# Batch setup in pieces, finer pacing of table work, and 512-column inverse groups with two accumulators in a fused attention and long-convolution kernel

## The chip, the cores and the metric

The kernel runs on one core of one Trainium2 chip. The metric is the device time of one execution in microseconds (us). Executions of one kernel on one chip agree within some 1%; three chips were used, and on two of them the kernel before is 0.5 to 0.9% slower than on the first (medians 3187.9, then 3214.7 to 3217.6, and 3204.8). So kernels are compared here by ratio to the kernel before in the same rounds, or stage by stage in the traces.

## The reference, cut to what matters

```python
def _attn_ref(u, v, z):                    # u, v: 8 x 3136 x 256, z: 8 x 3136 x 64
    scores = (1.0 / S) * np.matmul(z, z.transpose(0, 2, 1))
    attn = np.maximum(scores, 0.0) ** 2
    return u * np.matmul(attn, v)

def _moe_ref(x, w_proj, filter_fft, w_out):
    x1, x2, x3 = split(x @ w_proj)         # three parts of 256 columns
    X2 = np.fft.rfft(x2, n=S, axis=1)      # 1569 frequencies
    H = np.fft.rfft(filter_fft, n=S, axis=0)[None]
    y = x1 * np.fft.irfft(X2 * H, n=S, axis=1) * x3
    return y @ w_out                       # float32
```

The attention result is the x of the second function. Both Fourier transforms are done as matmuls with tables of cosines and sines, which the kernel makes itself while attention runs.

## The kernel before

A sequence of 3136 rows is 25 tiles of 128 rows (the last has 64) and 7 chunks of up to 512 columns (the last has 64). 1569 frequencies are 13 tiles (the last has 33 rows). The attention stage of a batch starts with a setup:

```python
for b in range(B):
    zT16 = batchp.tile([dqk, S], BF16, name="zT16")
    for t in range(NST):                                   # 25 tiles
        zsb = io.tile([P, dqk], F32, name="zblk")          # two buffers
        nc.sync.dma_start(out=zsb[:rows, :], in_=z[b, ds(t * P, rows), :])
        ptz = psA_pr.tile([P, CH], F32, name="ps_pr")
        nc.tensor.transpose(ptz[:dqk, :rows], zsb[:rows, :], ...)
        nc.vector.tensor_copy(zT16[:, ds(t * P, rows)], ptz[:dqk, :rows])
    # ... the same for u, two transposes per tile, copied by ScalarE
    # ... v: 25 loads on the GpSimd queue into the only buffer v16
```

Then come the chunks. After each, table work is given out in whole "slices": a slice is one band of 128 table rows, or the start or end of a group of four bands.

```python
    for c in range(NC):
        for kt in range(NST):
            nc.tensor.matmul(ps[...], zT16[...], zT16[...], start=True, stop=True)   # scores
            R = rring.tile([P, CH], F32, name="Rblk")
            nc.scalar.activation(R[...], ps[...], AF.Relu)
            if kt % ACT_SQUARE_EVERY == (ACT_SQUARE_EVERY - 1):      # every fourth
                nc.scalar.activation(A16[:krows, kt, :cw], R[...], AF.Square)
            else:
                nc.vector.tensor_tensor(A16[:krows, kt, :cw], R[...], R[...], ALU.mult)
            for dh in range(2):
                nc.tensor.matmul(psout[:, dh, :cw], v16[...], A16[:, kt, :cw], ...)
        # the gate: xT (name xTch) = psout * u, by VectorE; it ends the chunk
        # ... projections of xT, evicted by ScalarE and VectorE into ev tiles
        #     of two buffers (xiT, x2blk) and stored
        emit_table_slices(slices_per_chunk)   # one slice: done after 39 of 56 chunks
```

The inverse transform, for each half of four batches:

```python
CHI = 256
psB_i = phb.enter_context(tc.tile_pool(name="psB_i", bufs=1, space=PSUM))
for c in range(NCI):                          # 12 chunks of 256 columns, one of 64
    # ... loads itC on the sync queue and itS on the scalar queue, one DMA per
    #     frequency tile: 26 DMAs into pools of two buffers
    for bl in range(Bh):                      # 4 batches
        for dh in range(2):
            po = psB_i.tile([P, CHI], F32, name="psB_inv")
            for ft in range(NFT):             # 13: one accumulation group has 26 matmuls
                nc.tensor.matmul(po, Ac16[:fw, ft, ...], itC[:fw, ft, :cw], ...)
                nc.tensor.matmul(po, As16[:fw, ft, ...], itS[:fw, ft, :cw], ...)
            # gt = po * g1 and yT2 = gt * g3 by VectorE
        # ... output matmuls (psB_out), evicted by ScalarE (ostage), stored
```

## Time and profile before

| | kernel before |
|---|---|
| time, median of 5 runs | 3185.91 us (3182.3 to 3203.1) |
| attention with tables | 1580 us |
| forward transform and inverse, first half | 425 and 415 us |
| forward transform and inverse, second half | 336 and 428 us |

The whole-span line of busy times on the page of the kernel before is the place where one starts, and alone it misleads: PE (TensorE) looks like the bound everywhere and everything else like slack.

```profile
PE 2771.3 (87%) x15356; PEld 1356.8 (43%) x15356; DVE 1608.1 (51%) x3669; ACT 1327.4 (42%) x3400; POOL 132.4 (4%) x235
```

DVE is VectorE, ACT is ScalarE, POOL is GpSimd, PEld is the weight loads; each has its busy microseconds, share and number of instructions. The 51% of VectorE is an average over an attention stage where it is at 80% and two inverse stages where it is at 19%.

For finer comparisons this document marks the stages by instructions: attention ends at the last gate; an inverse is counted from its first to its last emptying of an accumulator (the instruction that writes gt); what lies between is put down to the forward transform. These marks give 1578.6, 435.7, 405.7, 346.3 and 412.5 us for the kernel before. The windows of the prediction (1580, 425, 415, 336, 428) count the filling of the first group into the inverse.

### The profile page before, as it was taken

The page shows a single profiled execution, that of the slowest core. Times are in us where ns is not written, and L with a number is a line of the kernel's source. Part 1 is how long each engine was busy: PE and PEld are TensorE (multiplying, and loading weights), DVE is VectorE, ACT ScalarE, POOL GpSimd, SP SyncE. Part 2 cuts the span into 40 slices and gives each one's busy share as a digit, 9 for nine tenths or more (in the row PEclk, how much of TensorE's full clock was granted, in tenths as well). Part 3 has the DMA queues.
Part 4 walks back from the last instruction along what each step waited for, and adds up shares of the span by engine and source line. Part 5 has one row for each costly group of instructions (what it writes and reads, how often), then busy time and mean ns, then how long its engine had stood idle before and what let it go on. Part 6 is the DMA issues. An engine that isn't in the chain of part 4 may idle for free.

```text
span 3183.3 us, 45398 instructions
## 1 busy us (share of the span) xinstructions
PE 2771.3 (87%) x15356; PEld 1356.8 (43%) x15356; DVE 1608.1 (51%) x3669; ACT 1327.4 (42%) x3400; POOL 132.4 (4%) x235
## 2 busy tenths in 40 slices
PE   8979979899798897989869999888888888888888
PEld 2333333333333332323334554566664333466666
DVE  8989988889989765655512222211111222311111
ACT  7879878788687775867600000000000000000000
POOL 2010010100101001010100000000000000000000
PEclk9989988899798899989979999999999999899999
DMA  4142243331332423222253221534344333234333
GB/s 91 61 110 82 87 91 109 69 123 44 87 107 64 111 61 59 66 50 69 62 132 58 49 57 26 142 108 122 106 111 130 61 61 61 60 102 120 107 108 82
DMA packets 552881, 271.08 MB, mean 85 GB/s; under 512 B 268236, under 2 KB 540104, under 8 KB 552648
## 3 DMA queue, kind: packets, MB, share of 16 engines
q1 hardware_dynamic: 352320, 200.91, 22.2%
q10 hardware_dynamic: 167960, 52.28, 7.3%
q0 software_dynamic: 32368, 14.99, 3.9%
q8 instruction: 120, 1.97, 0.3%
q14 instruction: 113, 0.93, 0.1%
HBM read 179.32 MB, written 103.59 MB: 89 GB/s over the span
## 4 chain that ended last, share of the span: by engine, by line
PE 68%; DMA 12%; ACT 8%; DVE 8%; issue 2%; ACTq 1%; SPq 0%; POOL 0%; DVEq 0%; POOLq 0%
PE psoutT L245 16%; PE psB_fwd L344 9%; PE psB_fwd L346 9%; PE ps_sc L234 9%; PE psB_inv L401 7%; PE psB_inv L403 6%; ACT Rblk L237 4%; DMA itC<-tabCi 3%; PE ps_pr L257 2%; DMA itS<-tabSi 2%; DVE gt L410 2%; DVE A L241 2%; PE pt_tab L167 2%; DMA zblk<-in_z_dram 2%; PE ps_pr L215 1%
## 5 line engine op out<-in xcount | busy, mean ns | idle before, releaser
L237 ACT ACTIVATE Rblk<-ps_sc 128x512 f32<-128x512 f32 (+2 forms) x1400 | 713.4, 546 | 201.9 <-PE ps_sc L234 190.7
L245 PE MATMUL psoutT<-A,v 128*128 128x512 bf16 (+1 forms) x2800 | 736.4, 368 | 29.5 <-DVE A L241 19.0
L241 DVE TENSOR_TENSOR A<-Rblk 128x512 bf16<-128x512 f32 (+2 forms) x1064 | 637.4, 621 | 182.4 <-ACT Rblk L237 173.5
L401 PE MATMUL psB_inv<-itC,Ac 128*128 128x256 bf16 (+2 forms) x2704 | 617.5, 273 | 85.7 <-DVE gt L410 81.2
L403 PE MATMUL psB_inv<-itS,As 128*128 128x256 bf16 (+2 forms) x2704 | 616.7, 273 | 2.2 <-DMA itS<-tabSi 2.0
L344 PE MATMUL psB_fwd<-x2h,bandc 128*128 128x512 bf16 (+2 forms) x1300 | 507.8, 391 | 66.7 <-DVE As L356 33.2
L346 PE MATMUL psB_fwd<-x2h,bands 128*128 128x512 bf16 (+2 forms) x1300 | 506.2, 389 | 0.0
L234 PE MATMUL ps_sc<-zT 64*128 64x512 bf16 (+2 forms) x1400 | 459.4, 368 | 41.1 <-ACT Rblk L237 30.6
L410 DVE TENSOR_TENSOR gt<-psB_inv,g 128x256 bf16<-128x256 f32 (+1 forms) x208 | 85.2, 410 | 669.3 <-PE psB_inv L403 601.7
L420 ACT ACTIVATE ostage<-psB_out 128x256 f32<-128x256 f32 (+1 forms) x200 | 76.8, 384 | 760.8 <-PE psB_out L418 484.6
L245 PEld LDWEIGHTS <-v 128*128 128x128 bf16 x2800 | 233.5, 101 | 313.7 <-issue 196.1
L355 ACT ACTIVATE Ac<-psB_fwd 128x512 bf16<-128x512 f32 (+1 forms) x52 | 31.0, 597 | 720.9 <-PE psB_fwd L346 704.7
L356 DVE CAST As<-psB_fwd 128x512 bf16<-128x512 f32 (+1 forms) x52 | 35.9, 691 | 578.3 <-ACT Ac L355 578.3
L403 PEld LDWEIGHTS <-As 128*128 128x128 bf16 (+1 forms) x2704 | 263.0, 100 | 128.0 <-issue 96.7
L401 PEld LDWEIGHTS <-Ac 128*128 128x128 bf16 (+1 forms) x2704 | 262.0, 99 | 105.3 <-issue 70.8
L234 PEld LDWEIGHTS <-zT 64*128 64x128 bf16 (+1 forms) x1400 | 104.1, 95 | 336.9 <-issue 281.3
L344 PEld LDWEIGHTS <-bandc 128*128 128x128 bf16 (+2 forms) x1300 | 130.3, 100 | 180.7 <-DMA bandc<-tabC 31.8
L346 PEld LDWEIGHTS <-bands 128*128 128x128 bf16 (+2 forms) x1300 | 130.1, 100 | 164.4 <-issue 45.5
L239 ACT ACTIVATE A<-Rblk 128x512 bf16<-128x512 f32 (+1 forms) x336 | 194.9, 580 | 1.5
L221 POOL DMA_DIRECT2D v<-in_v_dram x200 | 116.3, 639 | 1291.0 <-DVE xTch L250 915.2
L418 PE MATMUL psB_out<-wo,yT 128*128 128x256 bf16 (+1 forms) x400 | 97.0, 282 | 42.2 <-ACT ostage L420 40.7
L257 PE MATMUL ps_pr<-xTch,wp 128*128 128x512 bf16 (+1 forms) x448 | 120.0, 361 | 10.3 <-DVE xTch L250 3.9
(74 smaller groups left out, 2407.8 us busy)
## 6 DMA issues: line engine op xcount, KB each, us to landing
ublk<-in_u_dram SPq DMA_DIRECT2D x192, 128.0 KB
out_dram<-ostage SPq DMA_DIRECT2D x192, 128.0 KB
bands<-tabS ACTq DMA_DIRECT2D x576, 32.0 KB
bandc<-tabC SPq DMA_DIRECT2D x576, 32.0 KB
itC<-tabCi SPq DMA_DIRECT2D x288, 64.0 KB
itS<-tabSi ACTq DMA_DIRECT2D x288, 64.0 KB
v<-in_v_dram POOLq DMA_DIRECT2D x192, 64.0 KB, 3.1
x1T_d<-xiT SPq DMA_DIRECT2D x96, 128.0 KB
```

The source lines that it names most:

```text
L221: nc.gpsimd.dma_start(out=v16[:rows, t, :], in_=v[b, ds(t * P, rows), :])
L234: nc.tensor.matmul(ps[:krows, :cw], zT16[:, ds(kt * P, krows)], zT16[:, ds(s0, cw)], start=True, stop=True)
L237: nc.scalar.activation(R[:krows, :cw], ps[:krows, :cw], AF.Relu)
L239: nc.scalar.activation(A16[:krows, kt, :cw], R[:krows, :cw], AF.Square)
L241: nc.vector.tensor_tensor(A16[:krows, kt, :cw], R[:krows, :cw], R[:krows, :cw], ALU.mult)
L245: nc.tensor.matmul(psout[:, dh, :cw], v16[:, kt, ds(dh * P, P)], A16[:, kt, :cw], start=(kt == 0), stop=(kt == NST - 1))
L257: nc.tensor.matmul(pp[:, :cw], wp16[:, ksub, ds((comp * 2 + nb) * P, P)], xT[:, ksub, :cw], start=(ksub == 0), stop=(ksub == 1))
L344: nc.tensor.matmul(pacc[:fw, 0, cN, :cwN], bandc[:rows, t, :fw], x2h[:rows, t, ds(cN * CH, cwN)], start=(t == 0), stop=(t == NST - 1))
L346: nc.tensor.matmul(pacc[:fw, 1, cN, :cwN], bands[:rows, t, :fw], x2h[:rows, t, ds(cN * CH, cwN)], start=(t == 0), stop=(t == NST - 1))
L401: nc.tensor.matmul(po[:, :cw], Ac16[:fw, ft, ds(col0, P)], itC[:fw, ft, :cw], start=(ft == 0), stop=False)
L403: nc.tensor.matmul(po[:, :cw], As16[:fw, ft, ds(col0, P)], itS[:fw, ft, :cw], start=False, stop=(ft == NFT - 1))
L410: nc.vector.tensor_tensor(gt[:, :cw], po[:, :cw], g1[:, :cw], ALU.mult)
```

## The change

Its intent is to take the serial batch start off the path, to spread the table work evenly over attention, and to halve the number of accumulation groups in the inverse and free each from the wait for its predecessor. The core of the diff:

```diff
-        vpool = pha.enter_context(tc.tile_pool(name="vpool", bufs=1))
+        vpool = pha.enter_context(tc.tile_pool(name="vpool", bufs=2))
+        batchin = pha.enter_context(tc.tile_pool(name="batchin", bufs=2))
+        evy = pha.enter_context(tc.tile_pool(name="evy", bufs=4))   # x2blk
+        evx = pha.enter_context(tc.tile_pool(name="evx", bufs=4))   # xiT
 ... a band is now yielded in three parts: columns 0-511, 512-1023, the rest
-                    yield gen_band
+                    yield first
+                    yield (lambda f=gen_block: f(CH))
+                    if not last:
+                        yield fin
 ... setup of batch b+1, one piece of four tiles per chunk of batch b
+        NPACE = B * NC - 4                                  # 52
+        def setup_piece(b, tiles, g):
+            nc.sync.dma_start(out=zin[:, :nf, :], in_=z[b, r, :].rearrange("(t p) d -> p t d", p=P))
+            nc.sync.dma_start(out=uin[:, :nf, :], in_=u[b, r, :].rearrange("(t p) d -> p t d", p=P))
+            nc.gpsimd.dma_start(out=v16[:, t0:t0 + nf, :], in_=v[b, r, :].rearrange("(t p) d -> p t d", p=P))
+            # ... then the same transposes and copies as before, for four tiles
-                emit_table_slices(slices_per_chunk)
+                if b + 1 < B:
+                    setup_piece(b + 1, nxt, c)
+                k = b * NC + c + 1
+                want = min(3 * NST, ceil(3 * NST * k / NPACE))
+                emit_table_slices(want - emitted[0])
+                emitted[0] = want
 ... second half
-    CHI = 256
+    CHI = 512
-        psB_ff, psB_i and psB_o, one buffer each, open through both halves
+        psB_ff only in the first forward stage; in the inverse stage:
+                    psB_i = ph4.enter_context(tc.tile_pool(name="psB_i", bufs=2, space=PSUM))
+                    psB_o = ph4.enter_context(tc.tile_pool(name="psB_o", bufs=1, space=PSUM))
+                    if h == 1:                              # forward stage of the second half
+                        padp = ph3.enter_context(tc.tile_pool(name="padp", bufs=1))
+                        padt = padp.tile([P, 2 * CH], F32, name="padt")
+                        nc.vector.memset(padt[:, 0:1], 0.0)
-                            ost = outstage.tile([P, 2, D], F32, name="ostage")
+                            ost = outstage.tile([P, 4, D], F32, name="ostage")
```

The pad shifts the two band buffers of the second forward stage past the memory that the last inverse chunk's tables still hold, so that their loads may start before that inverse ends.

## The prediction

> **What bounds the kernel now.** I first cut the span into its five stages, with the table of stretches. The attention stage, with projections and table generation, ends at about 1580 us (the last chunk's gate is at 1578.6). Then come forward transform and inverse of the first half of the batches, and the same for the second half.
>
> ```profile
> core 0: us, PE busy (x) PEld busy (x) DVE busy (x) ACT busy (x) POOL busy (x), PEclk, DMA share, GB/s
> 0.00:1580.00 1580.00, 1391.83 (x6293) 511.93 (x6294) 1270.61 (x3022) 1215.39 (x3133) 120.00 (x212) 0.92 0.30 79
> 1580.00:2005.00 425.00, 369.74 (x1956) 194.22 (x1955) 90.61 (x113) 18.90 (x40) 12.36 (x24) 0.92 0.33 66
> 2005.00:2420.00 415.00, 349.49 (x2903) 257.84 (x2903) 79.88 (x218) 38.80 (x101) 0.00 (x0) 0.98 0.44 117
> 2420.00:2756.00 336.00, 299.87 (x1302) 129.91 (x1301) 87.03 (x101) 14.71 (x25) 0.00 (x0) 0.95 0.33 70
> 2756.00:3184.00 428.00, 360.41 (x2905) 262.88 (x2904) 79.98 (x218) 39.57 (x102) 0.00 (x0) 0.94 0.39 107
> ```
>
> The reader sees half of the time in attention, with no engine full over the whole stage, and 843 us in the two inverses, with VectorE and ScalarE nearly idle. Second, the same view in 50 us stretches shows that attention is three regimes, not one:
>
> ```profile
> 550.00:600.00 50.00, 48.80 (x248) 17.76 (x245) 47.70 (x116) 43.66 (x112) 0.00 (x0) 1.00 0.16 54
> 750.00:800.00 50.00, 47.93 (x213) 16.21 (x211) 47.06 (x108) 42.46 (x102) 0.00 (x0) 1.00 0.16 54
> 950.00:1000.00 50.00, 48.13 (x210) 16.09 (x209) 47.89 (x108) 44.42 (x105) 0.00 (x0) 1.00 0.14 48
> 1000.00:1050.00 50.00, 28.99 (x171) 14.28 (x169) 44.22 (x143) 29.55 (x105) 15.56 (x25) 0.57 0.55 121
> 1150.00:1200.00 50.00, 48.65 (x198) 15.31 (x198) 33.47 (x53) 40.68 (x82) 0.00 (x0) 1.00 0.11 35
> ```
>
> Where tables are made (up to about 1100 us) VectorE is 94 to 96% busy. A batch start (1000 to 1050) has PE at 29 of 50 and clock 0.57. After the tables are done (1150), VectorE has a third of its time free. Third, the timeline of VectorE gives the chunk period through the gate that ends each chunk (the instruction writing xTch); here the last small chunk of batch 6 and the first four chunks of batch 7:
>
> ```profile
> 1397.55 0.36 DVE L250 SCALAR_TENSOR_TENSOR xTch<-psoutT,uT 128x64 bf16<-128x64 f32 x2 [0.31 <-PE psoutT L245]
> 1445.72 1.28 DVE L250 SCALAR_TENSOR_TENSOR xTch<-psoutT,uT 128x512 bf16<-128x512 f32 x2
> 1471.44 1.29 DVE L250 SCALAR_TENSOR_TENSOR xTch<-psoutT,uT 128x512 bf16<-128x512 f32 x2 [0.28 <-PE psoutT L245]
> 1499.85 0.69 DVE L250 SCALAR_TENSOR_TENSOR xTch<-psoutT,uT 128x512 bf16<-128x512 f32 x1 [0.37 <-PE psoutT L245]
> 1522.78 1.28 DVE L250 SCALAR_TENSOR_TENSOR xTch<-psoutT,uT 128x512 bf16<-128x512 f32 x2
> ```
>
> The first chunk takes 48.2 us, a plain one 22.9. The cause stands in the PE timeline of the batch before: loads of z of one tile each, through two buffers, ahead of every transpose.
>
> ```profile
> 1227.31 0.39 PE L205 MATMUL ps_pr<-ident_f,zblk 128*64 128x128 f32 x1 [3.20 <-DMA zblk<-in_z_dram]
> 1228.14 0.39 PE L205 MATMUL ps_pr<-ident_f,zblk 128*64 128x128 f32 x1 [0.44 <-DVE zT L206]
> ```
>
> Fourth, for the inverse, the PE timeline at the end of an accumulation group:
>
> ```profile
> 2201.99 0.27 PE L403 MATMUL psB_inv<-itS,As 128*128 128x256 bf16 x1
> 2202.19 0.28 PE L401 MATMUL psB_inv<-itC,Ac 33*128 33x256 bf16 x1
> 2202.31 0.27 PE L403 MATMUL psB_inv<-itS,As 33*128 33x256 bf16 x1
> 2202.51 0.28 PE L418 MATMUL psB_out<-wo,yT 128*128 128x256 bf16 x1
> 2203.09 0.27 PE L401 MATMUL psB_inv<-itC,Ac 128*128 128x256 bf16 x1 [0.30 <-DVE gt L410]
> ```
>
> Matmuls start 0.11 us apart, lose about 0.1 us at each change to and from the 33-row block, and the next group waits for VectorE to empty the only accumulator.
>
> **What the Trainium skill says.**
> - "TensorE: Matmul & The Clock Gate", section "Back-to-back issue gap": a warm matmul of N columns follows the last after N / 2.4 + 2.5 ns, so 109 ns for 256 columns and 216 ns for 512. The trace agrees: 0.109 us in the inverse, 0.215 in attention. So wide matmuls win nothing per column; what they halve is the number of group ends.
> - The same page, section "Part 1: The HAM clock gate": a PE idle for some 3.4 us falls to half clock. The clock of 0.57 in the batch start above agrees.
> - "Perfetto Trace Analysis", section "Optimization Strategy": regimes with different busiest engines gain from being interleaved. That is the intent of the new pacing; the stretches at 950 and 1150 are two such regimes.
> - The same page, section "Matmuls": independent groups should rotate through PSUM banks so that the emptying of one overlaps the next. The 0.30 above and 0.52 us at the next group are that wait.
>
> **The change, part by part.**
>
> Attention, batch setup: z, u and v come four tiles per transfer, one piece per chunk of the batch before, with v in two buffers. The work of setup stays (600 fp32 transposes, 400 ScalarE and 200 VectorE copies); its serial wait goes, save for batch 0. The seven first chunks of batches 1 to 7 took 47.3, 49.1, 53.1, 52.3, 57.5, 46.7 and 48.2 us, together 354. If each becomes an ordinary chunk with its share of setup, about 27 us, this saves 354 - 7 x 27 = 165 us: 1579 - 165 = 1414.
>
> Attention, pacing: the same table work in thirds of a band over 52 chunks, not whole bands in the first 39 of 56. It removes no instruction. What bounds the evened stage is the sum per engine: VectorE 1270.6 us, at the 95.1% of the three full stretches (47.55 of 50), needs 1336; ScalarE 1215.4 at their 87.0% (43.51 of 50) needs 1397. The two counts are not added: they are two views of the same stage.
>
> Attention, output buffers of four: ScalarE and VectorE waited 35.8 and 9.3 us in the list of waits for stores of the projected tiles. Part of this comes back. Batch 0 keeps its start (first gate at 47.1 us), now with u queued between the z loads: about 10 us lost. I choose 1405 us, between the counts, saving 174.
>
> Forward stages: only the place of the filter accumulator and a 4 KB pad change, which keeps the band tiles clear of the larger inverse tables so that they still load early. 426 and 336 us stay.
>
> Inverse, per half: six chunks of 512 columns and one of 64, in place of twelve of 256 and one. Now a pair of groups takes 3.62 + 4.04 = 7.66 us: 2 x (26 x 0.109 + 0.20) + 4 x 0.109 = 6.5, and 1.16 of waits for the accumulator. With two accumulators the waits go: a pair at 512 columns is 2 x (26 x 0.216 + 0.20) + 8 x 0.109 = 12.5 us, a chunk of four batches 50.0, six of them 300. To this come:
> - the start: the first group needs all tables of its chunk, now 3.2 MB; at the 211 GB/s of 2010 to 2020 us that is 15 us, and the group ends some 2 us later, so about 11 us over the group's own 5.8. Now it is about 7 (first emptying 9.6 us after the first load).
> - the ends of chunks. Now the ScalarE queue issues 13 table loads at 0.5 to 0.65 us each when a chunk's tables come free, its evictions of the output stand behind them, and PE loses about 2 to 4 us: chunks are 32 to 34 us apart, not 30.6. I estimate 4 us for each of five larger bursts: 20.
> - the 64-column chunk, 12.6 us now (2407.4 to 2420.0): 12.
>
> Sum 343; with 3 more in the first half, where the band loads compete, and 1 at the very end, 346 and 344, for 415 and 428 now.
>
> Total: 1405 + 426 + 346 + 336 + 344 = 2857 us, a saving of about 328 us or 10%.
>
> **The rivals.**
> - *Setup stalls PE in order.* The transposes now stand inside full chunks, and share two PSUM buffers with the projections. If a load or a copy is late, scores behind it wait. For it: the PE order is fixed, and VectorE, which empties z, is nearly full. Against it: a piece has a whole chunk (25 us) for 1.2 MB, and the DMA share mid-batch is 0.14 to 0.16. Three microseconds in each of 48 chunks would make about 3000.
> - *The inverse turns its accumulator wait into a table wait.* The bytes of a burst double, and both issuing queues also carry the gates and outputs. For it: the DMA share at such a chunk end (2178 to 2189) is already 0.73. Against it: a chunk now lasts 50 us, and 7.6 MB in it is 152 GB/s. If bursts cost 12 us each, 40 us per half: about 2935.
> - *Better overlap than counted.* With VectorE at 95% from start to end attention takes 1340 to 1350, and with no chunk-end loss the inverses 325: about 2755.
>
> **Range and chances.** Attention I hold to within 55 us either way, the two inverses together to within 45; mostly independent, so about 75 around 2857, stretched upward for the PE stalls: 2775 to 2950. All three rivals stay faster by over 2% (3122 us); only both bad ones together, doubled, would reach it. Faster 0.97, same 0.02, slower 0.01.
>
> **What would show it.** Attention should end near 1405 with no first chunk over 35 us after batch 0, VectorE near 90% and ScalarE near 87% all along, no stretch of clock 0.57. If chunks are all longer with VectorE under 85%, the in-order rival holds. In the inverse the gap before a group for VectorE should fall from 81 us to almost nothing, groups should end about 5.8 to 6.7 us apart, and losses should sit at chunk ends alone. The forward stages should keep their length; a longer second forward stage would show that the pad fails and bands load late. The prediction is wrong if attention stays over 1480 or an inverse over 375.

## The result, and the profile after

The changed kernel takes 2863.39 us (median of 9 runs, 2857.99 to 2869.07); the kernel before took 3187.89 on that chip (16 runs, 3180.23 to 3203.44). The ratio is 0.8976, with a 95% interval of 0.8960 to 0.8992. A ratio is the mean time of one kernel's fast runs over that of the other's of the same rounds, so not quite the ratio of the medians quoted. It belongs to the first chip: the new attention takes the same time on all three (1418.5 to 1424.2 us), the old one took 14 us longer on the second, where the ratio would be some 0.891 (an estimate, under e1 and e2).

In the changed kernel the gate is line 292 (before 250), the inverse matmuls are 452 and 454 (401, 403), the emptying of an accumulator is 461 (410), the output matmul and its eviction are 469 and 471 (418, 420), the forward matmuls 393 and 395 (344, 346). The busy line of its page, and after it the table of its five stages (columns: stretch, its length, busy time and count of PE, PEld, DVE, ACT, POOL, then granted PE clock, DMA share and GB/s):

```profile
PE 2660.3 (93%) x12860; PEld 1102.4 (39%) x12860; DVE 1562.3 (55%) x3420; ACT 1336.4 (47%) x3458; POOL 58.7 (2%) x91
```

```profile
0.00:1420.00 1420.00, 1354.51 (x6292) 495.89 (x6293) 1254.69 (x2962) 1224.17 (x3190) 45.73 (x67) 0.97 0.33 88
1420.00:1846.00 426.00, 368.71 (x1958) 193.97 (x1955) 91.67 (x115) 19.32 (x41) 12.98 (x25) 0.92 0.33 66
1846.00:2184.00 338.00, 318.35 (x1656) 141.36 (x1656) 65.06 (x125) 38.99 (x101) 0.00 (x0) 0.99 0.49 145
2184.00:2520.00 336.00, 300.95 (x1300) 129.94 (x1300) 86.70 (x99) 14.92 (x25) 0.00 (x0) 0.94 0.32 69
2520.00:2857.00 337.00, 317.74 (x1656) 141.27 (x1656) 64.21 (x122) 38.98 (x101) 0.00 (x0) 0.98 0.45 134
```

The cuts stand where those of the kernel before stand, between the last matmul of a forward transform and the first of an inverse (1844.7 and 1847.0, 2518.4 and 2521.4).

| stage | before | predicted | after |
|---|---|---|---|
| attention | 1580 | 1405 | 1420 |
| forward, first half | 425 | 426 | 426 |
| inverse, first half | 415 | 346 | 338 |
| forward, second half | 336 | 336 | 336 |
| inverse, second half | 428 | 344 | 337 |

The reader sees that the engines' work in attention is nearly what it was (VectorE 1255 us for 1271, ScalarE 1224 for 1215) in 160 us less, and that the matmul count of an inverse fell from 2903 to 1656.

The timeline of VectorE of the changed kernel around a batch change, from the last full chunk of one batch over its small chunk to the first two of the next:

```profile
180.03 1.29 DVE L292 SCALAR_TENSOR_TENSOR xTch<-psoutT,uT 128x512 bf16<-128x512 f32 x2
192.91 0.35 DVE L292 SCALAR_TENSOR_TENSOR xTch<-psoutT,uT 128x64 bf16<-128x64 f32 x2 [0.38 <-PE psoutT L287]
223.03 1.29 DVE L292 SCALAR_TENSOR_TENSOR xTch<-psoutT,uT 128x512 bf16<-128x512 f32 x2 [0.48 <-PE psoutT L287]
250.23 1.28 DVE L292 SCALAR_TENSOR_TENSOR xTch<-psoutT,uT 128x512 bf16<-128x512 f32 x2
```

The first chunk of the batch takes 30.1 us (192.91 to 223.03), the next 27.2. It took 46.7 to 57.5 before. The stretches of 50 us of the changed kernel no longer show three regimes:

```profile
1150.00:1200.00 50.00, 49.08 (x216) 17.28 (x215) 46.10 (x103) 45.76 (x111) 0.00 (x0) 1.00 0.21 72
1250.00:1300.00 50.00, 49.02 (x225) 17.82 (x226) 41.95 (x110) 41.58 (x117) 0.00 (x0) 0.80 0.30 98
```

The stretch at 1150 us had VectorE at 33.47 of 50 in the kernel before; it has 46.10 now. The lowest clock of a 50 us stretch of attention after its start is the 0.80 of the second line; the 0.57 is gone. And the timeline of PE at an accumulation group's end in the inverse:

```profile
2013.53 0.38 PE L454 MATMUL psB_inv<-itS,As 128*128 128x512 bf16 x1
2013.84 0.39 PE L452 MATMUL psB_inv<-itC,Ac 33*128 33x512 bf16 x1
2014.07 0.38 PE L454 MATMUL psB_inv<-itS,As 33*128 33x512 bf16 x1
2014.38 0.28 PE L469 MATMUL psB_out<-wo,yT 128*128 128x256 bf16 x1
2014.50 0.38 PE L452 MATMUL psB_inv<-itC,Ac 128*128 128x512 bf16 x1
```

The bracket with the wait for gt, which stood at the start of the next group before, is gone: the next group starts 0.12 us after the output matmul. The 33-row block still costs about 0.1 us on entry and exit (0.31 us between starts instead of 0.22).

### The profile page after: what moved, and what is told of

It is laid out like the page before. It is cut to its first block, busy times and chain, and to the rows that moved or that the text cites. A ratio compares the mean times of both kernels' runs of the same rounds, so it can differ in the third digit from the quotient of the medians.

```text
span 2856.1 us, 38734 instructions
## 1 busy us (share of the span) xinstructions
PE 2660.3 (93%) x12860; PEld 1102.4 (39%) x12860; DVE 1562.3 (55%) x3420; ACT 1336.4 (47%) x3458; POOL 58.7 (2%) x91
## 5 line engine op out<-in xcount | busy, mean ns | idle before, releaser
L452 PE MATMUL psB_inv<-itC,Ac 128*128 128x512 bf16 (+3 forms) x1456 | 493.8, 356 | 5.4 <-DMA itC<-tabCi 5.4
L276 PE MATMUL ps_sc<-zT 64*128 64x512 bf16 (+2 forms) x1400 | 467.3, 365 | 33.3 <-ACT Rblk L279 26.7
L454 PE MATMUL psB_inv<-itS,As 128*128 128x512 bf16 (+3 forms) x1456 | 492.5, 354 | 3.3 <-DMA itS<-tabSi 3.1
L461 DVE TENSOR_TENSOR gt<-psB_inv,g 128x512 bf16<-128x512 f32 (+1 forms) x112 | 70.0, 625 | 533.8 <-PE psB_inv L454 490.6
L287 PEld LDWEIGHTS <-v 128*128 128x128 bf16 x2800 | 225.6, 101 | 271.6 <-issue 171.5
L452 PEld LDWEIGHTS <-Ac 128*128 128x128 bf16 (+1 forms) x1456 | 135.6, 98 | 181.6 <-issue 71.1
L454 PEld LDWEIGHTS <-As 128*128 128x128 bf16 (+1 forms) x1456 | 136.2, 98 | 109.3 <-issue 4.1
L256 PE MATMUL ps_pr<-ident_f,uin 128*128 128x128 f32 (+1 forms) x400 | 115.4, 314 | 11.6 <-DMA uin<-in_u_dram 4.9
L257 ACT ACTIVATE uT<-ps_pr 128x128 bf16<-128x128 f32 (+1 forms) x400 | 104.0, 277 | 40.0 <-PE ps_pr L256 35.9
```

The lines of the kernel that those rows point to most:

```text
L256: nc.tensor.transpose(ptu[:, :rows], uin[:rows, i, ds(dh * P, P)], ident_f32[:rows, :rows])
L257: nc.scalar.activation(uT16[:, dh, ds(t * P, rows)], ptu[:, :rows], AF.Copy)
L276: nc.tensor.matmul(ps[:krows, :cw], zT16[:, ds(kt * P, krows)], zT16[:, ds(s0, cw)], start=True, stop=True)
L287: nc.tensor.matmul(psout[:, dh, :cw], v16[:, kt, ds(dh * P, P)], A16[:, kt, :cw], start=(kt == 0), stop=(kt == NST - 1))
L452: nc.tensor.matmul(po[:, :cw], Ac16[:fw, ft, ds(col0, P)], itC[:fw, ft, :cw], start=(ft == 0), stop=False)
L454: nc.tensor.matmul(po[:, :cw], As16[:fw, ft, ds(col0, P)], itS[:fw, ft, :cw], start=False, stop=(ft == NFT - 1))
```

## The experiments

The theory at the start of the experiments was that of the prediction, sharpened by the traces: attention is bounded by the sum of VectorE's (and ScalarE's) work, and gains because that work is now spread; the inverse gains from fewer group ends and from the second accumulator. The rivals were that the two halves of the change act on each other, that the batch start alone is worth the gain in attention, that the smaller size of a table piece is what matters, and that width alone or the second accumulator alone makes the inverse. The stage marks of all runs, in us:

| kernel | attention | forward 1 | inverse 1 | forward 2 | inverse 2 | median | ratio to before |
|---|---|---|---|---|---|---|---|
| before | 1578.6 | 435.7 | 405.7 | 346.3 | 412.5 | 3187.9 | 1 |
| changed | 1419.4 | 439.3 | 323.7 | 350.7 | 318.5 | 2863.4 | 0.8976 |
| e1, inverse only | 1592.5 | 444.2 | 326.1 | 351.5 | 320.7 | 3034.9 | 0.9425 |
| e2, attention only | 1424.2 | 436.1 | 416.3 | 348.4 | 405.5 | 3040.8 | 0.9462 |
| e3, setup only | 1568.6 | 440.1 | 422.2 | 347.7 | 401.8 | 3197.7 | 0.9931 |
| e4, pacing only | 1501.6 | 436.4 | 423.8 | 348.3 | 417.3 | 3137.1 | 0.9742 |
| e5, one accumulator | 1418.5 | 442.2 | 360.6 | 350.4 | 352.4 | 2930.8 | 0.9154 |
| e6, 256 columns | 1421.7 | 435.5 | 359.1 | 345.3 | 354.7 | 2923.1 | 0.9129 |
| e7, no pad | 1420.5 | 442.5 | 321.6 | 382.4 | 320.2 | 2888.6 | 0.9021 |
| e8, store buffers two | 1452.0 | 444.1 | 326.3 | 348.0 | 319.2 | 2893.2 | 0.9026 |
| e9, whole bands spread | 1437.5 | 445.1 | 323.9 | 347.7 | 318.9 | 2878.1 | 0.8948 |
| e10, thirds in 39 chunks | 1521.6 | 442.6 | 327.2 | 351.5 | 320.7 | 2968.6 | 0.9236 |
| e11, bf16 relu | 1364.1 | 442.5 | 324.7 | 346.2 | 319.4 | 2808.2 | 0.8733 |
| e12, best | 1357.1 | 442.1 | 317.4 | 304.8 | 308.1 | 2740.2 | 0.8523 |

The intervals of the ratios are about 0.003 either way. e1 to e4 and e9 to e12 ran on a second chip, e5 to e8 on a third. All results were correct. Stages whose code a run leaves alone show how far a mark moves by itself: up to 14 us for the old attention (1592.5 in e1 for 1578.6 on the first chip) and 5 for the new, up to 18 us for the old inverse (423.8 in e4 for 405.7) and 4 us for the new.

### e1 and e2: each half of the change alone

```diff
 e1: attention as in the kernel before, from "Bh = B // 2" on as in the changed kernel
 e2: attention as in the changed kernel, from "Bh = B // 2" on as in the kernel before
```

> Attention as before, the inverse stages (512 columns, two accumulators, pad) as changed. If the gains of the stages simply add: each inverse 333 to 337 us as in the changed kernel, against 415 and 428 before, the forwards within 4 us of before, the whole about 3012 us (3000 to 3025), attention unmoved at 1579. The rival, that the inverse gained from the new attention (tables or gates placed or written differently): one of the inverses stays above 350 and the whole above 3035.

> Attention as changed, forwards and inverses as before. If the gains add: attention 1415 to 1425 us, inverses back to 415 and 428, the whole about 3030 us (3015 to 3045). The rival as in the run before would show inverses under 400.

Measured: 3034.86 us (ratio 0.9425) and 3040.78 us (0.9462). The product of the ratios is 0.892, the whole change has 0.8976. In e1 the inverses take 326 and 321 us as in the changed kernel, and in e2 attention takes 1424 us as in the changed kernel. So the two halves add up stage by stage, and nothing is given back between them. e1's time lies 10 us above its expected range, at the edge of its rival's 3035; the trace shows why, for the old attention is 14 us longer on that chip, and both inverses are far under the rival's 350. The product is 0.6% lower than the whole, and that too is the chip: e9, which ran there and differs from the changed kernel only by whole bands, has 0.8948 with attention 13 us longer than in e2, so the changed kernel should have some 0.891 there (an estimate).

### e3: the setup in pieces alone

```diff
+        vpool bufs=2, batchin, batch_tiles() and setup_piece() as in the change
         (evx and evy with bufs=2, the old table slices, the old inverse)
+                if b + 1 < B:
+                    setup_piece(b + 1, nxt, c)
                 emit_table_slices(slices_per_chunk)
```

> Before plus only the batched and early loads and transposes of the next batch; tables in whole bands in the first 39 chunks, store buffers of two. My theory (the serial setup is the larger loss, but without pacing the chunks with tables stay bound by VectorE): VectorE work of the first 39 chunks about 1024 us at 95% is 1077, the other 17 chunks about 385, so attention about 1480, the whole 3085 us (3065 to 3105), and first chunks of batches no longer 47 to 57 us. The rival, that pacing brought the gain: attention over 1530 and the whole over 3135.

Measured: 3197.69 us, ratio 0.9931 (0.9906 to 0.9955). The expected time was some 3085. Attention ends at 1568.6 us; the run with the old attention on the same chip, e1, ends it at 1592.5, so the setup in pieces by itself is worth 24 us (22 by the ratio), not 165. Where the gain went can be seen in two stretches, the 39 chunks after which no table work is left (cut at the gate of the 39th) and the 17 after them. The kernel before:

```profile
0.00:1163.00 1163.00, 1018.61 (x4607) 378.41 (x4608) 1028.28 (x2560) 915.92 (x2411) 92.57 (x160) 0.90 0.33 88
1163.00:1579.00 416.00, 372.78 (x1683) 133.27 (x1682) 241.67 (x460) 298.59 (x719) 26.51 (x50) 0.96 0.23 56
```

The same two stretches of e3:

```profile
0.00:1192.00 1192.00, 1057.35 (x4644) 389.25 (x4645) 1024.99 (x2518) 944.76 (x2492) 39.42 (x59) 0.89 0.33 89
1192.00:1569.00 377.00, 358.79 (x1645) 127.09 (x1644) 236.92 (x447) 294.81 (x694) 5.03 (x7) 0.98 0.19 49
```

With the serial starts gone, the 39 chunks with table work take longer than before: 1192 us for 1163 (1171 in e1, on e3's chip). The first chunks of batches 1 to 7 did gain, together 253 us for 362 in e1, but the other chunks after the very first took 1266 for 1184. The starts had not been idle time for VectorE: at 1000 to 1050 us of the kernel before it was busy for 44 us, some 40 of them with table work, while PE was at 29. Take the wait away and the same table work stands in the other chunks, which grow; the gates of e3 show the full chunks of one batch at 38.7 and 40.1 us, where the kernel before had 31 to 35:

```profile
501.49 1.29 DVE L277 SCALAR_TENSOR_TENSOR xTch<-psoutT,uT 128x512 bf16<-128x512 f32 x2 [0.24 <-PE psoutT L272]
540.22 1.29 DVE L277 SCALAR_TENSOR_TENSOR xTch<-psoutT,uT 128x512 bf16<-128x512 f32 x2
580.34 1.29 DVE L277 SCALAR_TENSOR_TENSOR xTch<-psoutT,uT 128x512 bf16<-128x512 f32 x2
```

Only in the tail, where VectorE has room, does the removal show (377 us, for 416 before and 422 in e1).

One rival is left here. e3 has two store buffers, and VectorE waits for the stores of xiT for 15.0 us of its first 1116 (up to 5.2 at a time; 0.4 us in the first 1110 of the kernel before), and its first chunks of batches 1 to 5 still take 36 to 43 us. e8 shows the same waits. The setup in pieces with four buffers and the old table slices was not run; with e8's 32 us on top it would be worth some 56 (an estimate), a third of 165.

### e4: the pacing alone

```diff
-                    yield gen_band
+                    (thirds of a band, as in the change; setup and inverse as before)
-                emit_table_slices(slices_per_chunk)
+                want = min(3 * NST, ceil(3 * NST * k / NPACE))
+                emit_table_slices(want - emitted[0])
```

> Before plus only the tables in thirds over 52 chunks; setup serial as before. My theory: first chunks of batches still 45 us and more, the other chunks evened to 26 us, attention 1530 to 1550, the whole about 3145 us (3130 to 3160). The rival, that pacing brought the gain: attention under 1480, the whole under 3090.

Measured: 3137.07 us, ratio 0.9742. The whole is in its expected range; attention takes 1501.6 us, 91 less than e1's and below the 1530 to 1550 expected. The first chunks of batches still take 45.6 to 56.7 us, the other full ones 23 to 29. The stretch with table work in e4, to the last copy of a table block:

```profile
0.00:1318.00 1318.00, 1194.05 (x5554) 443.03 (x5555) 1175.92 (x2925) 1052.99 (x2707) 103.23 (x185) 0.95 0.33 87
```

VectorE is at 89% in it. Setup and pacing alone give 24 and 91 us; both, with the store buffers of e8, give 168 (1592.5 to 1424.2 in e2). So the two support each other: from e4 to e8 (1452.0 us), which differ in attention by the setup alone (but ran on two chips), the setup is worth 50 us, twice what it is without the pacing. A reading that fits, though no run isolates it, is that evened table work leaves less to fill the batch starts with.

### e5 and e6: the two parts of the inverse

```diff
 e5:
-                    psB_i = ph4.enter_context(tc.tile_pool(name="psB_i", bufs=2, space=PSUM))
+                    psB_i = ph4.enter_context(tc.tile_pool(name="psB_i", bufs=1, space=PSUM))
 e6:
-    CHI = 512
+    CHI = 256
```

> The changed kernel with one inverse accumulator in place of two, still 512 columns. If the accumulator wait is paid per group end: 112 groups in all at 0.58 us (the loss per group before, 1.16 us a pair) plus about 0.27 us for the longer emptying (0.69 us against 0.42) make 80 to 95 us more: 2950 us (2935 to 2965). The rival, that widening to 512 columns alone brought most of the inverse gain: under 2900.

> The changed kernel with 256 columns in place of 512, still two accumulators. If the second accumulator brought most of the gain: a pair 2 x (26 x 0.109 + 0.20) + 0.44 = 6.5 us, a chunk of 256 columns 26.1, half 0.9 us above half a 512 chunk, and 11 chunk ends a half of 2 us: about 30 us a half over the changed kernel at most, the whole 2890 to 2925 us. The rival, widening brought most: over 2960.

Measured: 2930.8 us (0.9154) and 2923.08 us (0.9129). e6 lies inside its range, at its upper edge; e5 is a few us below its range of 2935 to 2965. The waits of PE in the first inverse, each line with the sum in us, the count and the longest; first the kernel before, then e5, then the changed kernel:

```profile
PE psB_inv L401 <- DVE gt L410: 40.6, 99, 0.8
```

```profile
PE psB_inv L452 <- DVE gt L461: 29.7, 44, 0.8
```

```profile
PE psB_out L469 <- ACT ostage L471: 13.5, 10, 5.0
PE psB_out L469 <- DVE yT L462: 2.2, 2, 2.0
PE psB_inv L454 <- DMA itS<-tabSi: 1.3, 4, 0.6
PE psB_inv L452 <- DMA itC<-tabCi: 0.4, 1, 0.4
```

With one accumulator the wait for gt is back, half as often as before because there are half as many groups. A pair of groups lasts, from one emptying to the next but one, 7.66 us for 256 columns in the kernel before (3.62 + 4.04), 6.65 in e6 (3.05 + 3.60), 14.12 in e5 (6.65 + 7.47) and 12.55 in the changed kernel (5.82 + 6.73). Per 512 columns that is 15.3, 13.3, 14.1 and 12.55. Over both halves the marked inverses sum to 818 us before (822 to 841 in e2 to e4, on the second chip), 714 with two narrow accumulators, 713 with one wide one, 642 with both. Each part alone saves about 105 us, both 176: they overlap, for each removes group-end waits that the other would remove too, and either rival ("it is the width", "it is the second accumulator") falls.

### e7: the pad

```diff
-                    if h == 1:
-                        padp = ph3.enter_context(tc.tile_pool(name="padp", bufs=1))
-                        padt = padp.tile([P, 2 * CH], F32, name="padt")
-                        nc.vector.memset(padt[:, 0:1], 0.0)
```

> The changed kernel without the 4 KB pad. If the pad keeps the band tiles clear of the inverse tables: the bands of the second forward stage load only when the last inverse tables of the first half are free, the second forward starts 5 to 15 us late, 339 us become 345 to 355, the whole 2870 to 2880. The rival, that the pad does nothing: within 4 us of the changed kernel.

Measured: 2888.58 us, ratio 0.9021 (0.8992 to 0.9049), and a second forward stage of 382.4 us, where the three other runs of that call have 345 to 350. The expectation was 5 to 15 us. The waits of PE in e7 at the start of that stage name the cause, in one piece:

```profile
PE psB_fwd L389 <- DMA bandc<-tabC: 30.9, 1, 30.9
```

The first band tile comes 31 us late, once; the changed kernel has no such line in that stage. The stage lost 32 us by the trace. The whole kernel, by its ratio, lost only 0.0045 of the time before (some 14 us), but that ratio divides by a kernel before that is 17 us slower on e7's chip, while the new attention is as fast there as on the first. The profiled runs settle it: e7's span is 35.8 us longer than the changed kernel's (2891.9 for 2856.1), and 32 of them are in this stage.

### e8: two store buffers instead of four

```diff
-        evy = pha.enter_context(tc.tile_pool(name="evy", bufs=4))
-        evx = pha.enter_context(tc.tile_pool(name="evx", bufs=4))
+        evy = pha.enter_context(tc.tile_pool(name="evy", bufs=2))
+        evx = pha.enter_context(tc.tile_pool(name="evx", bufs=2))
```

> The changed kernel with two buffers, not four, for the projected tiles that wait for their stores. Before, ScalarE and VectorE waited 45 us in all for these stores. If half of that was on the path: 15 to 30 us more, 2880 to 2893. If the engines that wait there have time to spare: within 8 us of the changed kernel.

Measured: 2893.19 us, ratio 0.9026; attention 1452.0 us, 30 to 34 more than in the three other runs on that chip. The waits of e8 in attention that the changed kernel doesn't have:

```profile
ACT xiT L303 <- DMA x1T_d<-xiT: 34.3, 14, 6.3
DVE xiT L305 <- DMA x1T_d<-xiT: 24.9, 8, 5.9
PE ps_pr L312 <- ACT xiT L303: 19.2, 7, 5.3
```

With two buffers the eviction waits for the store of the tile before the last, up to 6 us at a time, and PE behind it waits for the eviction. The place is the batch change: the first chunks of batches 1 to 5 take 34 to 39 us in e8, for 27 to 30 in the changed kernel. So the buffers are a third term in attention, at the upper edge of what was expected. The prediction had left it at "part of this comes back"; it is worth about 32 us. Going from the old attention of e1, the terms read: setup 24 us, pacing 91, store buffers 32, and 26 that only setup and pacing together give; sum 173, to 1419. (The store buffers are taken from e8 on another chip; where code is equal the chips' marks of the new attention differ by at most 6 us.)

### e9 and e10: size of a table piece, or evenness?

```diff
 e9:
-                want = min(3 * NST, ceil(3 * NST * k / NPACE))
+                want = 3 * min(NST, ceil(NST * k / NPACE))      # whole bands, over 52 chunks
 e10:
-        NPACE = B * NC - 4
+        NPACE = 39                                              # thirds, over 39 chunks
```

> The changed kernel, but the three thirds of a band are emitted together, so whole bands, spread over the same 52 chunks. If it is the size of the piece that matters (a whole band's chain of some 40 VectorE instructions goes ahead of the next chunk's squares, and PE starves behind it): chunks with a band 36 to 40 us as with the setup alone, the others 25 to 26, attention 1530 to 1570, the ratio to before 0.93 to 0.945. If it is the even spread over more chunks: attention near 1440, the ratio under 0.91.

> The changed kernel with the thirds paced over the first 39 chunks in place of 52. If it is the size of the piece that matters: the first 39 chunks 28 to 30 us, the later full ones 25, attention 1450 to 1470, the ratio to before 0.905 to 0.915. If it is the spread: first 39 chunks over 33 us, attention over 1530, the ratio over 0.93.

Measured: 2878.06 us, ratio 0.8948 (0.8919 to 0.8977), for e9; 2968.59 us, ratio 0.9236, for e10. In e9 attention takes 1437.5 us, as expected if evenness matters (near 1440; 1530 to 1570 if the size of the piece does), 13 us longer than in e2 on the same chip. e10 lies between its two expectations (1450 to 1470 for size, over 1530 for the spread), nearer to the second: with the same thirds given out over 39 chunks instead of 52, attention takes 1521.6 us, 97 longer than in e2. So evenness matters, and the size of the piece hardly. The stretches with and without table work in e10:

```profile
0.00:1150.00 1150.00, 1041.64 (x4617) 379.47 (x4617) 1013.49 (x2462) 942.85 (x2508) 40.57 (x59) 0.92 0.34 92
1150.00:1522.00 372.00, 357.18 (x1676) 128.86 (x1676) 242.49 (x469) 303.64 (x715) 5.21 (x8) 1.00 0.20 53
```

And the stretch with table work in the changed kernel:

```profile
0.00:1340.00 1340.00, 1278.43 (x5919) 468.26 (x5920) 1202.96 (x2857) 1160.27 (x3034) 45.42 (x66) 0.96 0.34 90
```

VectorE is at 88% where e10 makes tables and at 65% where it doesn't, over 372 us. In the changed kernel it is at 90% over 1340 us, with only 80 us of tail. Up to the last copy of a table block the share is 89.3% (before, 1124 us), 86.4% (e3, 1171), 89.2% (e4, 1318), 88.0% (e10, 1163), 89.3% (e9, 1323), 87.2% (e8, 1380) and 89.7% (changed, 1348): whatever the order of the work, VectorE doesn't get past about 90% over a long stretch, and the two that fall short have the setup in pieces with two store buffers. As a description, the length of attention is about VectorE's work over 0.9, plus the share that a tail leaves unused.

A count from PE's side fits as well, and no run separates the two. It is worked out from the packed traces: take PE's busy time in attention from each trace, and from it take the time lost to the half clock (one less the granted share, summed over the busy time). All kernels run the same 6288 matmuls there:

| kernel | attention, us | PE idle | lost to the clock | rest |
|---|---|---|---|---|
| before | 1579 | 187 | 91 | 1300 |
| e1, old attention | 1593 | 192 | 106 | 1294 |
| e3, setup only | 1569 | 153 | 111 | 1305 |
| e4, pacing only | 1502 | 146 | 53 | 1303 |
| e10, thirds in 39 | 1522 | 123 | 82 | 1316 |
| e8, store buffers two | 1452 | 84 | 68 | 1300 |
| e9, whole bands spread | 1438 | 74 | 47 | 1317 |
| changed | 1420 | 65 | 44 | 1310 |
| e11, bf16 relu | 1364 | 47 | 13 | 1304 |

The rest is nearly the same in all, so attention is some 1305 us of matmuls at full clock plus what PE idles and what it loses to the clock. PE's ends are modelled, so the split is rough; that the rest stays within 2% while attention varies by 17% speaks for it. Of the 159 us that the change saves here, about 122 are idle time and 47 clock (the rest grew by 10). It also says how far reordering can go: the changed kernel is within some 110 us of the time that its own matmuls take (an estimate from this table). In the changed attention PE waits 26.7 us for ScalarE's relu and only 3.0 for VectorE's squares (30.6 and 19.0 before). And the clock did not come back with the serial starts: e3, without them, lost as much as e1.

### e11: less work on VectorE and ScalarE

```diff
-ACT_SQUARE_EVERY = 4
+ACT_SQUARE_EVERY = 64                  # no square on ScalarE
-                    R = rring.tile([P, CH], F32, name="Rblk")
+                    R = rring.tile([P, CH], BF16, name="Rblk")
```

> The changed kernel with the relu result in bf16, not fp32, and all squares on VectorE. If VectorE and ScalarE together bound the attention stage: a square falls from 0.69 to about 0.36 us, so VectorE needs about 21 us a full chunk (15.3 - 19 x 0.29 + 6 x 0.36 + 9.4), ScalarE about 20, PE 22, and chunks go from 26.5 to about 24, attention from 1420 to about 1290, the ratio to before about 0.857 (0.845 to 0.87). If PE or waiting in order bounds it: less than 40 us, the ratio over 0.885.

Measured: 2808.19 us, ratio 0.8733; attention 1364.1 us, 60 less than e2's. Expected were 1290 us and 0.857 (0.845 to 0.87), so it lies outside. The result stayed correct. The group of squares in e11, between 300 and 600 us, and then its stretch with table work:

```profile
L283 DVE TENSOR_TENSOR A<-Rblk 128x512 bf16<-128x512 bf16 x249 | 100.7, 419 | 13.0 <-ACT Rblk L279 9.4
```

```profile
0.00:1200.00 1200.00, 1160.51 (x5576) 446.47 (x5577) 1065.12 (x3224) 945.12 (x2447) 43.49 (x66) 0.99 0.37 100
```

A square from bf16 took 419 ns, from fp32 686; I had estimated 360. All squares on VectorE cost 517 us (1400 of them) where 1064 had cost 634, so 117 us less; but the builder, which chooses the engine of each copy of a transposed table block, now put 269 of them on VectorE instead of 107, and these cost 57 us instead of 23. VectorE's busy time in attention falls by 102 us, from 1255 to 1153 (84 by these two, the rest because neighbouring records overlap more), ScalarE's by 167, from 1224 to 1057. ScalarE's share in the stretch with tables drops from 87 to 79%, VectorE's stays at 88.8%: relieved together, ScalarE was left with free time, VectorE was not. That speaks for VectorE rather than ScalarE; it doesn't rule out PE, for against e2 the loss to the clock fell by 38 us and PE's idle time by 18. Both the square's estimate and the copies are parts of the miss. A third is the tail, now 164 us, whose chunks without table work take 24.2 us, not less than the 22.9 of the kernel before, at VectorE 54% and ScalarE 68%. What fills such a chunk can be read from the starts of PE's instructions, here in e11 (x2 is two matmuls in one line):

```profile
1319.94 0.59 PE L287 MATMUL psoutT<-A,v 128*128 128x512 bf16 x2
1320.46 0.39 PE L276 MATMUL ps_sc<-zT 64*128 64x512 bf16 x1
1320.79 0.59 PE L287 MATMUL psoutT<-A,v 128*128 128x512 bf16 x2
1321.32 0.39 PE L276 MATMUL ps_sc<-zT 64*128 64x512 bf16 x1
```

Two matmuls into psoutT start 0.22 us apart, but 0.31 to 0.33 us pass where the rows change between the 64 of a score and the 128 of a second matmul. Gaps of PE over 0.1 us sum to only 0.7 us of the 24.2 (0.6 of the 22.9). In e11's order such a chunk has 36 changes, in the kernel before 28: eight more, at about 0.1 us each, are most of the 1.3 us. So PE's own stream fills these chunks.

### e12: a version that beats both

```diff
 e11, and:
-        psB_f = phb.enter_context(tc.tile_pool(name="psB_f", bufs=1, space=PSUM))
+                    psB_f = ph3.enter_context(tc.tile_pool(name="psB_f", bufs=1 if h == 0 else 2, space=PSUM))
-                    psB_o = ph4.enter_context(tc.tile_pool(name="psB_o", bufs=1, space=PSUM))
+                    psB_o = ph4.enter_context(tc.tile_pool(name="psB_o", bufs=2, space=PSUM))
 table loads of an inverse chunk: 8 DMAs of up to four frequency tiles, all on
 the sync queue, in place of 26 of one tile on the sync and scalar queues
+                            for it, tab in ((itC, tabCi), (itS, tabSi)):
+                                nc.sync.dma_start(out=it[:, f0:f0 + nf, :cw],
+                                                  in_=tab[ds(f0 * P, nf * P), ds(s0, cw)].rearrange("(t p) s -> p t s", p=P))
```

> The run before, and in the inverse two output accumulators and the tables in 8 transfers of up to 512 KB, all on SyncE's queue, so that ScalarE's evictions no longer stand behind table loads; and two forward accumulators in the second half[...]. Expected from the waits in the changed kernel: 33 us less in the second forward stage (339 to 306), the chunk ends of the inverses from about 2 us each to almost nothing, 20 us in all: about 50 us faster than the run before, the ratio about 0.016 lower. If larger loads make the gates wait behind them on the one queue, the inverses stay at 334 or grow.

Measured: 2740.17 us, ratio 0.8523 (0.8501 to 0.8545), the fastest of all: 0.021 below e11 where 0.016 (50 us) had been expected. The stages that it touches: second forward 346.2 to 304.8 us (41 where 33 were expected), inverses 324.7 to 317.4 and 319.4 to 308.1. Ahead of it, the trace of the changed kernel had this line among the waits of PE in the second forward stage:

```profile
PE psB_fwd L393 <- DVE As L405: 33.2, 12, 2.8
```

Twelve times, once between each two of the 13 frequency tiles, PE waited 2.8 us for the one accumulator to be emptied. With two there is no such line in e12. The ends of inverse chunks, which cost 1.7 us each in the changed kernel (8.25 to 8.75 us between emptyings over such an end, 6.74 inside), cost nothing in e12 (6.75 to 6.91). Fewer table DMAs, their move off ScalarE's queue and the second output buffer were tried together, so which of them did it is open.

## Why the prediction was right, and which steps failed

The predicted total, 2857 us, is 6 us from the measured median. That is closer than its terms deserve, and partly luck, for two of them missed in opposite directions: attention was 15 us too low, the inverses together 15 us too high.

1. **Attention, the count by batch starts: right in place, wrong in what it needs.** The step "If each becomes an ordinary chunk with its share of setup, about 27 us, this saves 354 - 7 x 27 = 165 us" came out at 1414 for 1420, and the gates show it where it was put: the first chunks of batches 1 to 7 take 199.5 us (189 counted), the other chunks after the very first 1170 for 1177. What failed is that the setup alone would do this. In e3 it saves 24 us, because the other chunks grow by what the first ones lose. The step overlooked what its own evidence showed: in the batch start at 1000 to 1050 us PE was at 29 of 50 but VectorE at 44.22. A wait of PE in which VectorE works off what must be done anyway is only gained when that work is spread. Nor does this trace show the idle time of 3.4 us that the prediction cites from the Trainium skill for the clock gate: the half clock was granted from 1006.8 to 1054.6 us, and PE had idled only 1.5 us when it set in.
2. **Attention, the count by engines: right in kind, its share too high, and not the only one that fits.** The 95.1% came from three of the best stretches; no kernel holds it over a stage. Over its whole stretch with tables the kernel before had 89.3%, and 1270.6 / 0.893 = 1423 us would have been the count (an estimate after the fact, which leaves out the tail). The 87.0% for ScalarE met the 86.2% measured, but e11 shows that ScalarE isn't the limit: its share fell to 79% and VectorE's stayed. The prediction left PE out: busy for 1354.5 of the 1420 us, its matmuls are a floor of some 1305, and a part of the gain came through the clock. Which of VectorE and PE sets the 1420 is not shown.
3. **Pacing as "thirds of a band over 52 chunks": half right.** Over 52 chunks, yes (97 us between e10 and e2); thirds, hardly (13 us between e9 and e2).
4. **Store buffers: not sized.** About 32 us by e8. The prediction's 1405 contained it only through the count by engines, which is why it could be left open without harm.
5. **Batch 0: mis-sized.** "About 10 us lost" was about 3; the first gate came at 50.3 us, for 47.1 before.
6. **Inverse, pair of groups: right.** 12.5 predicted, 12.55 measured; the wait for gt went from 40.6 us in the first half to none.
7. **Inverse, ends of chunks: mis-sized.** The term "I estimate 4 us for each of five larger bursts: 20" measured about 1.7 us at four of the ends, 7 in all. The fifth, before the small chunk, cost nothing. With it 301 (24 pairs) + 7 + 16 (start of the first half; 11 in the second) + 14 (the small chunk; 18 with the very end in the second half) are the measured 338 and 337. The waits of PE behind ScalarE's evictions of the output, 13.5 us in the first half, are what is left at these ends. The larger bursts didn't cost more than the small ones, so the rival of a table wait fell: all waits of PE for itC and itS in the first inverse sum to 3.8 us.
8. **Forward stages: right.** 426 and 336, as predicted. That the pad is what keeps the second at its length is shown by e7, at 32 us in the stage.
9. **The rival of setup stalling PE in order: fell.** No first chunk after batch 0 is over 30.1 us, and PE's idle time ahead of its setup transposes for u sums to 11.6 us on the page, 4.9 of it for the loads.

## What to carry to other kernels

Before counting a wait as a gain, look at what the busiest engine does in that stretch: if it is filling the wait with work that must be done anyway, removing the wait moves the work and saves nothing until the work is spread or cut. Count a stage as the work of its busiest engine over the share that this engine held over a whole regime, not over its best stretches, set beside it the other engines that come near full and the clock that they were granted, and spread side work over as much of the stage as there is, for the size of the pieces matters little. Two changes that remove the same kind of wait (wider groups, a second accumulator) don't add up, so measure each alone before crediting either.

## What the Trainium skill lacked or had wrong

- "TensorE: Matmul & The Clock Gate", section "Back-to-back issue gap", gives about 131 ns per matmul as the sustained figure for streams of weight load and matmul at 512 columns, and calls N / 2.4 + 2.5 ns an isolated gap that over-counts. In both kernels the streams of pairs at 512 columns start 0.21 to 0.22 us apart (2012.88, 2013.10, 2013.32, 2013.53 in the changed inverse), with a weight load for each. The formula holds for the stream; the sustained figure wasn't seen.
- "VectorE: DVE Perf Modes", section "The perf-mode tier table", gives a bf16 tensor_tensor about twice the speed of fp32, for 2048 elements. At 512 elements the square took 419 ns against 686, 1.64 times. The page's own fixed term of some 150 cycles, in its section on the TRN2 errata, accounts for it: put into it, 256 cycles give an estimate of (256 + 151) / 0.96 = 424 ns. The table would need a second column for small tiles.
- No page gives the cost of a change of row count inside a stream of matmuls: going from 128-row to 33-row weights and back cost about 0.1 us each way (starts 0.31 us apart at 512 columns where 0.22 is usual, 0.20 where 0.11 is usual at 256), and so do the changes between 64-row scores and 128-row matmuls in attention (0.31 to 0.33).
- No page that I found warns that a wait of one engine can be the time in which the busiest engine catches up: taking the batch starts away left the 39 chunks with tables at 1192 us, for 1163 before.
